# One crossbar transpose per chunk pair of q, in a planned attention and MLP kernel

## The chip, the cores and the metric

The kernel runs on one core of one Trainium2 chip. The metric is device time in microseconds (us) of one launch. The core has a matrix engine (TensorE, PE in the profile, with its weight loads as PEld), a vector engine (DVE), a scalar engine (ACT), GpSimd (POOL), and a sync engine (SP) that here only issues transfers. Sixteen DMA engines move the data. Each engine runs its own instructions strictly in order and waits on semaphores for the others.

## The reference

A block-wise decaying linear attention, followed by a two-layer MLP whose activation is a smooth ReLU. In short:

```
for each block of 64 positions of a sequence (4 batches, 8 heads, 768 positions, head size 64):
    out   = ((q k^T) * lam^(i-j), lower triangle) v  +  (q * lam^(i+1)) state
    state = lam^64 * state + (k * lam^(63-i))^T v
x = out, as (3072 tokens, 512)
h = x @ w_in                        # 512 -> 2048
g = 0 if h <= -1, h if h >= 1, else (h + 1)^2 / 4
y = g @ w_out                       # 2048 -> 512, float32
```

## The kernel before

**Attention.** The kernel works on 24 chunks c of 128 tokens, 6 in each batch, and gathers four chunks into a stripe of 512 tokens, 6 stripes in all. q is loaded for a pair m of chunks at once (`lq`, 512 KB, line 460), with the pair's 256 tokens dealt alternately to two halves e = 0 and 1. k and v are loaded for one chunk at a time (`ld`, 256 KB each, line 464). GpSimd multiplies q and k by powers of lam and casts them to bf16: `cq` (m, e) by `cast_q` (line 244) and `cast` (c, 1) by `cast` (line 240); the casts of k for the first four chunks are on the vector engine. The scalar engine casts v (`cast` (c, 2), line 259).

For the score product, q and k are needed with the head dimension on the partitions. For the first pairs (m below 3) and chunks (c below 6) TensorE transposes them (`tq`, `t`). For the other 9 pairs and 18 chunks a crossbar DMA issued from SP does: `f_qx` (line 288) issues one of 512 columns for each half e of a pair, 18 in all, into `qT`, and `f_kx` (line 284) one for each chunk of k into `kT`, also 18.

Then, for a chunk, TensorE computes the scores `s` (lines 309 to 315), the vector engine masks them (`m`, line 317), and TensorE computes the output `o` (lines 326 to 335) from the masked scores and the running state. `u` (line 291) adds the chunk to the state, from the cast k and v alone. ACT copies the state (`ub`) and the output (`x`, line 337).

**MLP.** `l1` (lines 347 to 368) multiplies a stripe with w_in, `r` (ACT, line 370) and three vector operations `g` (lines 378, 381 and 386) make the activation, and `l2` (line 391) multiplies with w_out: for each of the four chunks `ms` of a stripe, four groups `kg` of four matmuls of 512 columns, accumulated in one tile. `la` are the first four l1 of the first stripe, over the 384 tokens that are there first. `y` (ACT, line 410) copies a finished tile, and `st` (line 427) stores it. The last tile of the kernel is cut into two column parts.

**Order.** Nothing in the order is left to the hardware. All operations are given to a small list planner (`run_plan`, lines 178 to 227) with an estimated duration, the operations that they need, and a due time. It plays the program through by these estimates and writes each engine's instructions in the order that it finds. So a changed estimate, or a changed list of needs, moves instructions on every engine. The estimates are only used for the order. l2 of a stripe is woven between the l1 of the next (lines 430 to 443). For the last stripe there is no next l1, and its sixteen l2 groups run one after another.

**Transfers.** SP issues all loads of q, k and v, all crossbar transposes and all stores through one queue. The weights go through GpSimd's queue (`w`, lines 155 and 159), in eight transfers of 512 KB. By lines 478 to 500 some transfers wait for a weight transfer to land, so the weights and the first chunks take turns.

**Tiles.** `qs` (the cast q) has one tile for each half, from the pool `qkp` with 4 buffers; `ks` has another 4 there. `qT` is one tile for a pair, with 3 buffers. The program tracks which instruction must wait for which by the tiles' addresses.

Of the kernel before, what the change touches and what calls it, by code (L numbers as in the profile page):

```python
# [9 lines left out]
BF16 = mybir.dt.bfloat16  # L10
# [5 lines left out]
def _bc(ap, idx, n):  # L16

    a = list(ap.ap)
    a = a[:idx] + [[0, n]] + a[idx:]
    return bass.AP(ap.tensor, ap.offset, a)  # L20
# [3 lines left out]
def kernel(  # L24
# [16 lines left out]
    nc = tc.nc  # L41
    B, H, S, D = q.shape
# [7 lines left out]
    FO = d_ff // 128  # L50
    MS = 512
    NST = n_tok // MS
    NCH = n_tok // C
    CPS = MS // C

    LD = 6
    LQ, NQ2 = 3, 3
# [13 lines left out]
    lq = ctx.enter_context(tc.tile_pool(name="lq", bufs=LQ))  # L71
    qtq = ctx.enter_context(tc.tile_pool(name="qtq", bufs=NQ2))
    qkp = ctx.enter_context(tc.tile_pool(name="qkp", bufs=NQK))
    qtp = ctx.enter_context(tc.tile_pool(name="qtp", bufs=NQT))
    scp = ctx.enter_context(tc.tile_pool(name="scp", bufs=3))
    xp = ctx.enter_context(tc.tile_pool(name="xp", bufs=3))
# [33 lines left out]
        out=causal, in_=causal, compare_op=AX.is_ge, fill=0.0,  # L110
# [52 lines left out]
    LAT, FILL = 70, 170  # L163
    FAR, SLACK, XSL = 8, 5000, 2000
# [9 lines left out]
    def add(key, eng, ns, fn, needs=(), due=None, extra=0, dma=0, perf=False):  # L174
        OPS[key] = Op(key, eng, ns, fn, needs, due, extra, dma, perf)
        ops.append(OPS[key])

    def run_plan(free):

        users = {x.key: [] for x in ops}  # L180
        for x in ops:
            x.needs = [OPS[y] for y in x.keys if y in OPS]
            for y in x.needs:
                users[y.key].append(x)
        left = {x.key: len(x.needs) for x in ops}
        topo = [x for x in ops if not x.needs]
        for x in topo:
            for u in users[x.key]:
                left[u.key] -= 1
                if left[u.key] == 0:  # L190
                    topo.append(u)
        assert len(topo) == len(ops)
        for x in reversed(topo):
            d = [u.due - u.ns - x.extra - LAT for u in users[x.key] if not u.dma]
            x.due = min(d + ([x.own] if x.own is not None else []), default=1e9)
            if x.dma or x.key[0] in ("l1", "l2"):
                x.due = x.own
        left = {x.key: len(x.needs) for x in ops}
        ready = {e: [] for e in free}
        for x in topo:  # L200
            if not x.needs:
                ready[x.eng].append((0, x))
        out_seq, xfer, dma_free = [], [0] * RING, 0
        while len(out_seq) < len(ops):
            t, e = min((max(free[e], min(r for r, _ in lst), xfer[-RING] if e == "SP" else 0), e)
                       for e, lst in ready.items() if lst)
            r, x = min(((r, x) for r, x in ready[e] if r <= t), key=lambda p: (p[1].due, p[0]))
            ready[e].remove((r, x))
            ns = x.ns + (720 if x.perf and free["POOL"] > t else 0)
            free[e] = t + ns  # L210
            x.t, x.end = t, t + ns + x.extra
            if x.dma:
                dma_free = max(dma_free, t + (1300 if e == "SP" else 2100)) + x.dma
                x.end = dma_free + 1400
                if x.key[0] in ("ld", "lq") and x.key[1] >= (FAR if x.key[0] == "ld" else FAR // 2):
                    x.end += SLACK if (x.key[1] if x.key[0] == "ld" else 2 * x.key[1]) >= 10 else NEAR
                if e == "SP":
                    xfer.append(dma_free)
            out_seq.append((t, len(out_seq), x))
            for u in users[x.key]:  # L220
                left[u.key] -= 1
                if left[u.key] == 0:
                    ready[u.eng].append((max(y.t if y.eng == u.eng and y.key != u.gate else y.end + (XSL if u.eng == "SP" and y.eng == "POOL" and u.dma == 640 else LAT) for y in u.needs), u))
        for t, _, x in sorted(out_seq, key=lambda p: p[:2]):
            if DBG:
                print(f"{t / 1e3:9.3f} {x.due / 1e3:9.3f} {x.eng:5s} {x.ns:6.0f} {x.key}")
            x.fn()

    def mm(*cols):
        return sum(c / 2.4 + 3 for c in cols)  # L230


    qs, ks, kT, qT, sc_sb, xT, ptt, pst, pot = {}, {}, {}, {}, {}, {}, {}, {}, {}
# [8 lines left out]
        eng.tensor_tensor(ks[c], qkv_ld[c, 1], _bc(tab_k[:, c % NCB, :], 2, D), op=AX.mult)  # L242

    def cast_q(m, e, eng):
        qs[m, e] = qkp.tile([128, H, D], BF16, name="qs", tag="qs")
        eng.tensor_tensor(qs[m, e], qkv_ld[m, 0][:, :, e], _bc(tab_q[:, e, m % (NCB // 2), :], 2, D), op=AX.mult)  # L246

    def qT_tile(m):
        if m not in qT:
            qT[m] = qtq.tile([128, 2, HP, 128], BF16, name="qT", tag="qT")  # L250
        return qT[m]
# [33 lines left out]
        kT[c] = qtp.tile([128, HP, 128], BF16, name="kT", tag="kT")  # L285
        nc.sync.dma_start_transpose(out=kT[c], in_=ks[c].rearrange("p h d -> p (h d)"))

    def f_qx(m, e):
        nc.sync.dma_start_transpose(out=qT_tile(m)[:, e], in_=qs[m, e].rearrange("p h d -> p (h d)"))  # L289

    def f_u(c):
        if c % NCB == 0:
# [140 lines left out]
    for s in range(1, NST + 1):  # L433
        n = PARTS.get(s, 1)
        l1 = [(1, s, i, p) for p in range(n) for i in range(0, FO, n)]
        l2 = [(ms, kg) for ms in range(CPS) for kg in range(CPS)]
        if s == 1:
            l2 = [(ms, kg) for kg in range(CPS) for ms in range(2)] + l2[FO // 2:]
        for i in range(FO):
            l_seq.append((2, s - 1) + l2[i])  # L440
            if s < NST:
                l_seq.append(l1[i])
# [26 lines left out]
    def f_w(it, wait):  # L469
        (load_w_in, load_w_out)[it[0]](it[1])  # L470
        if wait is not None:
            tc.add_manual_dep(w_dma[-1].ins, w_dma[wait].ins.name, SYNC)
# [5 lines left out]
    for it in order:  # L478
        if isinstance(it, tuple):
            prev = order[order.index(it) - 1]  # L480
            gated = len(w_seen) - 1 - prev % 2 if w_seen and isinstance(prev, int) else None
            need = [("w",) + w_seen[-1], ("cast", CPS - 1, 1) if len(w_seen) > 1 else None] if w_seen else \
                [("cast", CPS - 2, 2), ("cast", CPS - 2, 1)]
            if gated is not None:
                need.append(("w",) + w_seen[gated])
            add(("w",) + it, "POOL", 900, lambda it=it, wait=gated: f_w(it, wait), need, due=pos_ * 1e-3,
                dma=2560)
            if gated is not None:
                OPS[("w",) + it].gate = ("w",) + w_seen[gated]
            w_seen.append(it)  # L490
            pos_ += 1
            continue
        gated = len(w_seen) - 2 if last_c is not None and w_seen and not isinstance(order[order.index(it) - 1], int) else None
        for x in (1, 2) if it % 2 else (1, 0, 2) if it == 0 else (0, 1, 2):
            need = [("w",) + w_seen[-2] if w_seen else None]
            if x == 0:
                add(("lq", it // 2), "SP", 700, lambda i=it, wait=gated: f_load(i, 0, wait),
                    [("cq", it // 2 - LQ, 0), ("cq", it // 2 - LQ, 1)] + need, due=pos_ * 1e-3, dma=1850)
            else:
                add(("ld", it, x), "SP", 590, lambda i=it, x=x, wait=gated if x == 1 and i % 2 else None: f_load(i, x, wait),  # L500
                    [("cast", it - LD, x)] + need, due=pos_ * 1e-3, dma=1190)
            pos_ += 1
        last_c = it

    for c in range(NCH):
        od, cb = o_due(c), c % NCB
        lastu = c - 1 if cb else c - 2
        m = c // 2
        e = "DVE" if c < CPS else "POOL"
# [4 lines left out]
        for i in range(2 if c % 2 == 0 else 0):  # L514
            old = ("tq", m - NQK // 2, i)
            add(("cq", m, i), "POOL", 1060, lambda m=m, i=i: cast_q(m, i, nc.gpsimd),
                [("lq", m), ("cq", m, 0) if i else None, old, ("qT",) + old[1:]])
            if m < XQ:
                add(("tq", m, i), "PE", mm(*[128] * 4), lambda m=m, i=i: f_tq(m, i),
                    [("cq", m, i)] + ([("kT", c - 1), ("m", c - 1, 1), ("tq", m, 0) if i else None] if c >= CPS else []),  # L520
                    due=od - 6000, extra=FILL)
                add(("qT", m, i), "ACT", 600, lambda m=m, i=i: f_qT(m, i), [("tq", m, i)])
            else:
                add(("qT", m, i), "SP", 1200, lambda m=m, i=i: f_qx(m, i), [("cq", m, i), ("o", 2 * (m - NQ2) + 1)], due=-2, dma=640)
        if c < XT:
            add(("t", c), "PE", mm(*[128] * 4), lambda c=c: f_t(c),
                [("cast", c, 1), ("kT", c - 1), ("kb", c - 1, 0), ("kb", c - 1, 1), ("m", c - 1, 1) if c > 3 else None,
# [1 line left out]
                due=od - 6000, extra=FILL)  # L529
# [33 lines left out]
    for n1, (_, s, i, p) in enumerate(l1_order):  # L563
# [3 lines left out]
        j = (i // n) % rw  # L567
# [12 lines left out]
    for n2, (_, s, ms, kg) in enumerate(l2_order):  # L580
# [5 lines left out]
        y = s * CPS + ms  # L586
        add(("l2", n2), "PE", mm(*[512] * 4) if (s, ms) != LAST else mm(*[CUT if kg < 2 else d_model - CUT] * 8), lambda a=(s, ms, kg): f_l2(*a),
            need + [("w", 1, kg), ("l2", n2 - 1), ("y", y - 2) if kg == 0 else None], due=l_due[2, s, ms, kg], extra=FILL)
        if (s, ms) == LAST:
            if kg % 2:  # L590
                i = kg // 2
# [37 lines left out]
```

## Time and profile before

| | |
|---|---|
| median of 6 runs | 224.32 us (223.78 to 226.22) |
| the profiled execution, its time | 224.35 us |
| its span, first to last instruction | 222.7 us |
| TensorE matmul busy | 206.3 us, 93% |
| vector, scalar, GpSimd busy | 146.3, 124.0, 62.8 us |
| q transposes by DMA | 18, median 4.3 us from issue to landing |
| k transposes by DMA | 18, median 3.5 us from issue to landing |
| loads of k, of q, of v | 24, 12, 24; median 5.2, 5.4, 5.3 us to landing |

The profile has a page of one execution, and answers to queries of its trace. A row of the timeline gives the start in us, the duration, the engine, the line, the operation with the tile written and those read, how many were merged, and in brackets how long the engine had been idle and who ended the wait. "SPq" is SP's queue of transfers; the time of its row is that of issuing, and the landing is told apart. A row of the table of windows gives the busy time of each engine in a stretch, the granted TensorE clock, the mean busy share of the DMA engines, and GB/s. The share can come out a little over 1.

### The profile page before, as it was taken

What the parts mean: (1) busy time and instruction counts of PE and PEld (TensorE: products, weight loads), DVE (VectorE), ACT (ScalarE), POOL (GpSimd) and SP (SyncE); (2) the same over time, 40 slices, a digit from 0 to 9 for tenths busy, and PEclk for the clock granted to TensorE, in tenths of its full rate; (3) what the DMA queues carried; (4) which work ended last, traced back from release to release, by engine and by line L of the source; (5) the groups of instructions that cost most, each with busy time, mean ns of one, the idle gap of its engine ahead of it and who ended that gap; (6) DMA issues with size and microseconds to landing.
All of it is one profiled execution on the core that took longest, in us unless ns stands there. A gap on an engine that the chain in (4) does not pass through costs nothing.

```text
span 222.7 us, 4691 instructions
## 1 busy us (share of the span) xinstructions
PE 206.3 (93%) x1904; PEld 135.9 (61%) x1904; DVE 146.3 (66%) x218; ACT 124.0 (56%) x221; POOL 62.8 (28%) x65
## 2 busy tenths in 40 slices
PE   0587997999998999999999999999999999999993
PEld 0375544668577877776766766777767644444442
DVE  4577299989947875978477659995565564554301
ACT  3464868547547676657657465677645544455120
POOL 7371074217615360915141037520000000000000
PEclk9999999999999999999999999999999999999999
DMA  5999999999699999999999999984101101110212
GB/s 132 242 201 191 188 243 215 183 208 240 102 245 170 200 207 195 174 213 151 218 157 340 213 234 268 187 190 97 65 29 50 43 4 50 47 47 9 85 53 93
DMA packets 89974, 34.40 MB, mean 154 GB/s; under 512 B 70368, under 2 KB 87008, under 8 KB 89952
## 3 DMA queue, kind: packets, MB, share of 16 engines
q1 hardware_dynamic: 85584, 29.89, 66.6%
q0 software_dynamic: 4224, 4.19, 11.7%
q8 instruction: 15, 0.25, 0.5%
q14 instruction: 7, 0.06, 0.1%
q10 hardware_dynamic: 144, 0.00, 0.0%
HBM read 27.27 MB, written 6.29 MB: 151 GB/s over the span
## 4 chain that ended last, share of the span: by engine, by line
PE 67%; DMA 24%; SPq 4%; POOL 2%; issue 1%; DVE 0%; POOLq 0%
PE py L405 30%; PE ph L362 27%; DMA x0f<-in_q_dram 9%; DMA w_out_sb<-in_moe_w_out_dram 7%; DMA w_in_sb<-in_moe_w_in_dram 5%; PE po L334 3%; SPq L464 3%; PE ps L314 2%; DMA kT<-ks 2%; PE po L331 1%; POOL qs L246 1%; PE pu L295 1%; PE py L399 1%; POOL w_in_sb L155 1%; SPq L289 1%
## 5 line engine op out<-in xcount | busy, mean ns | idle before, releaser
L370 ACT ACTIVATE r<-ph,one 128x512 bf16<-128x512 f32 (+2 forms) x96 | 64.8, 679 | 54.3 <-PE ph L362 34.9
L362 PE MATMUL ph<-xT,w_in_sb 128*128 128x128 bf16 (+2 forms) x880 | 94.0, 255 | 0.2 <-ACT r L370 0.2
L405 PE MATMUL py<-w_out_sb,gT 128*128 128x512 bf16 x368 | 92.1, 379 | 0.0
L362 PEld LDWEIGHTS <-w_in_sb 128*128 128x128 bf16 x880 | 65.4, 98 | 23.3 <-issue 1.0
L378 DVE TENSOR_SCALAR t<-r 128x1024 bf16<-128x1024 bf16 x48 | 29.8, 621 | 38.7 <-ACT r L370 38.7
L405 PEld LDWEIGHTS <-gT 128*128 128x128 bf16 x368 | 33.9, 98 | 31.4 <-DVE gT L386 0.2
L386 DVE TENSOR_TENSOR gT<-w,t 128x1024 bf16<-128x1024 bf16 x48 | 40.3, 839 | 1.7
L381 DVE TENSOR_TENSOR w<-r,t 128x1024 bf16<-128x1024 bf16 x48 | 38.3, 797 | 1.3
L246 POOL TENSOR_TENSOR qs<-x0f,tab_q 128x512 bf16<-128x512 f32 x24 | 28.4, 1203 | 33.9 <-DMA x0f<-in_q_dram 29.0
L242 POOL TENSOR_TENSOR ks<-x1f,tab_k 128x512 bf16<-128x512 f32 x20 | 24.5, 1230 | 40.4 <-DMA x1f<-in_k_dram 19.6
L324 DVE TENSOR_TENSOR sc<-ps,causal 128x512 bf16<-128x512 f32 x20 | 13.7, 687 | 12.1 <-PE pt L314 12.1
L410 ACT COPY osb<-py 128x512 f32<-128x512 f32 x23 | 13.5, 586 | 12.3 <-PE py L405 10.4
L341 ACT CAST xT<-po 128x512 bf16<-128x512 f32 x24 | 14.1, 587 | 10.6 <-PE po L334 5.4
L334 PE MATMUL po<-sc,vi 128*128 128x128 bf16 x192 | 18.5, 222 | 0.6 <-DVE sc L322 0.5
L260 ACT CAST vi<-x2f 128x512 bf16<-128x512 f32 x24 | 14.8, 618 | 5.0 <-DMA x2f<-in_v_dram 4.9
L299 ACT CAST ubd<-pu 64x256 bf16<-64x256 f32 x40 | 14.6, 365 | 5.2 <-PE pu L295 4.9
L334 PEld LDWEIGHTS <-vi 128*128 128x128 bf16 x192 | 14.8, 100 | 3.4 <-issue 1.4
L331 PE MATMUL po<-qT,ubd 128*128 128x128 bf16 x80 | 14.6, 219 | 0.5 <-ACT xT L341 0.5
L324 DVE TENSOR_TENSOR sc<-pt,causal 128x512 bf16<-128x512 f32 x20 | 13.6, 680 | 0.0
L265 PE MATMUL pt<-ident,ks 128*128 128x128 bf16 x24 | 2.8, 248 | 7.4 <-DVE ks L242 7.2
L331 PEld LDWEIGHTS <-ubd 128*128 128x128 bf16 x80 | 7.8, 98 | 1.6
L314 PE MATMUL ps<-qT,kT 64*128 64x128 bf16 x80 | 7.9, 219 | 0.9 <-DMA kT<-ks 0.9
(55 smaller groups left out, 87.9 us busy)
## 6 DMA issues: line engine op xcount, KB each, us to landing
x1f<-in_k_dram SPq DMA_DIRECT2D x24, 256.0 KB, 5.2
x0f<-in_q_dram SPq DMA_DIRECT2D x12, 512.0 KB, 5.4
x2f<-in_v_dram SPq DMA_DIRECT2D x24, 256.0 KB, 5.3
out_dram<-osb SPq DMA_DIRECT2D x23, 256.0 KB, 2.5
w_in_sb<-in_moe_w_in_dram POOLq DMA_DIRECT2D x4, 512.0 KB, 9.1
w_out_sb<-in_moe_w_out_dram POOLq DMA_DIRECT2D x4, 512.0 KB, 8.6
qT<-qs SPq DMA_TRANSPOSE x18, 4.3
kT<-ks SPq DMA_TRANSPOSE x18, 3.5
```

The costliest lines, as they stand in the source:

```text
L242: eng.tensor_tensor(ks[c], qkv_ld[c, 1], _bc(tab_k[:, c % NCB, :], 2, D), op=AX.mult)
L246: eng.tensor_tensor(qs[m, e], qkv_ld[m, 0][:, :, e], _bc(tab_q[:, e, m % (NCB // 2), :], 2, D), op=AX.mult)
L260: nc.scalar.copy(out=v_out(vi[c % NV]), in_=qkv_ld[c, 2].rearrange("p (a b) d -> p a b d", b=2))
L324: nc.vector.tensor_tensor(sc_sb[c][:, g], pst[c, g], _bc(causal, 1, HP), op=AX.mult)
L331: nc.tensor.matmul(po[:, hp], lhsT=ubd[(c - 1) % NUB][:, hp, :], rhs=q_cols(c, hp), start=True, stop=False)
L334: nc.tensor.matmul(po[:, hp], lhsT=vi[c % NV][:, hp, hi].rearrange("p a d -> p (a d)"), rhs=sc_sb[c][:, hi, hp, :], start=(cb == 0 and hi ...
L362: nc.tensor.matmul(ph[:, j * m:(j + 1) * m], lhsT=w_in_sb[:, ko, (ni + j) * 128:(ni + j + 1) * 128], rhs=xT[s][:, ko, part * m:(part + 1) ...
L370: nc.scalar.activation(out=r_t[grp][:, i, cs], in_=ph_t[s, ni, part][:, cs], func=AF.Relu, bias=one[:, 0:1])
L378: nc.vector.tensor_scalar(t_t[grp], r, 0.5, 1.0, op0=AX.mult, op1=AX.min)
L381: nc.vector.tensor_tensor(w_t[grp], r, t_t[grp], op=AX.subtract)
L386: nc.vector.tensor_tensor(gT[s][:, f - RW * n:f, part * m:(part + 1) * m], w_t[grp].rearrange("p a (b m) -> p (a b) m", m=m), t_t[grp].rea ...
L405: nc.tensor.matmul(py_t[s, ms], lhsT=gT[s][:, ko, ms * 128:(ms + 1) * 128], rhs=w_out_sb[:, ko, :], start=(ko == 0), stop=(ko == FO - 1))
```

## The change

Four edits are made together.

1. The two halves of a pair's cast q lie in one tile, `qs[m]`, of a new pool `qsp` with 2 buffers. One crossbar DMA of 1024 columns transposes both halves, in place of two of 512. It needs the second half's cast, and is planned with 2000 ns of issue and 1280 ns of transfer, where each of the two had 1200 and 640. The planner's allowance between a GpSimd cast and a transpose of q or k, `XSL`, holds for the new size too.
2. The planner's `need` of the first weight transfer names the cast of the second half of q's pair 1, where it named the casts of k and v of chunk 2. What the transfer itself waits for on the chip is not set by this list.
3. In the last stripe, the first eight l2 groups come in the order (0,0), (0,1), (0,2), (1,0), (1,1), (1,2), (0,3), (1,3), where it was (0,0) to (0,3) and then (1,0) to (1,3).
4. Through the planner, the order of the instructions changes on PE, ACT, DVE and SP. On GpSimd it stays as it was.

```
+    qsp = ctx.enter_context(tc.tile_pool(name="qsp", bufs=2))
...
-... (XSL if u.eng == "SP" and y.eng == "POOL" and u.dma == 640 else LAT) ...
+... (XSL if u.eng == "SP" and y.eng == "POOL" and u.dma in (640, 1280) else LAT) ...
...
     def cast_q(m, e, eng):
-        qs[m, e] = qkp.tile([128, H, D], BF16, name="qs", tag="qs")
+        if e == 0:
+            qs[m] = qsp.tile([128, 2, H, D], BF16, name="qs", tag="qs")
+        qs[m, e] = qs[m][:, e]
...
-    def f_qx(m, e):
-        nc.sync.dma_start_transpose(out=qT_tile(m)[:, e], in_=qs[m, e].rearrange("p h d -> p (h d)"))
+    def f_qx(m):
+        nc.sync.dma_start_transpose(out=qT_tile(m).rearrange("p e h j -> p (e h) j"), in_=qs[m].rearrange("p e h d -> p (e h d)"))
...
+        if s == NST:
+            l2 = [(0, 0), (0, 1), (0, 2), (1, 0), (1, 1), (1, 2), (0, 3), (1, 3)] + l2[FO // 2:]
...
-                [("cast", CPS - 2, 2), ("cast", CPS - 2, 1)]
+                [("cq", CPS // 2 - 1, 1)]
...
-                add(("qT", m, i), "SP", 1200, lambda m=m, i=i: f_qx(m, i), [("cq", m, i), ("o", 2 * (m - NQ2) + 1)], due=-2, dma=640)
+                if i:
+                    add(("qT", m, 1), "SP", 2000, lambda m=m: f_qx(m), [("cq", m, 1), ("o", 2 * (m - NQ2) + 1)], due=-2, dma=1280)
```

More of the change, by code (lines that the diff above doesn't have):

```diff
@@ L222, in run_plan @@
                 if left[u.key] == 0:
-                    ready[u.eng].append((max(y.t if y.eng == u.eng and y.key != u.gate else y.end + (XSL if u.eng == "SP" and y.eng == "POOL" and u.dma == 640 else LAT) for y in u.needs), u))
+                    ready[u.eng].append((max(y.t if y.eng == u.eng and y.key != u.gate else y.end + (XSL if u.eng == "SP" and y.eng == "POOL" and u.dma in (640, 1280) else LAT) for y in u.needs), u))
         for t, _, x in sorted(out_seq, key=lambda p: p[:2]):
```

## The prediction

> **What bounds the kernel now.** I read the page's busy times first, then the table of windows, to see where TensorE is not the bound.
>
> ```profile
> PE 206.3 (93%) x1904; PEld 135.9 (61%) x1904; DVE 146.3 (66%) x218; ACT 124.0 (56%) x221; POOL 62.8 (28%) x65
> ```
> ```profile
> 36.00:60.00 24.00, 23.74 (x250) 15.59 (x250) 21.81 (x30) 14.40 (x27) 10.61 (x10) 1.00 1.05 194
> 60.00:70.00 10.00, 9.28 (x125) 7.02 (x123) 5.64 (x10) 6.05 (x11) 3.36 (x4) 1.00 0.99 181
> 70.00:148.00 78.00, 78.00 (x864) 56.94 (x862) 60.19 (x81) 49.29 (x88) 30.58 (x26) 1.00 1.11 210
> 148.00:205.00 57.00, 57.00 (x390) 33.19 (x389) 32.60 (x53) 30.70 (x51) 1.04 (x1) 1.00 0.18 53
> ```
>
> The first figure is the window's length, the second TensorE's busy time, the last three the granted clock, the DMA engines' share and GB/s. From 70 us on TensorE never idles at the full clock, so time is gained only ahead of that, and lost wherever a new wait appears. The DMA engines are full until about 148 us, so a late landing is the wait to fear. TensorE's timeline gives the idle times that can go, and the instructions that come just after their data:
>
> ```profile
> 20.89 0.27 PE L334 MATMUL po<-sc,vi 128*128 128x128 bf16 x2 [0.50 <-DVE sc L322]
> 34.41 0.38 PE L272 MATMUL pt<-ident,qs 128*128 128x128 bf16 x4 [0.67 <-ACT qT L278]
> 53.31 0.39 PE L295 MATMUL pu<-vi,ks 128*128 128x128 bf16 x4
> 59.40 0.23 PE L314 MATMUL ps<-qT,kT 64*128 64x128 bf16 x1 [0.21 <-DMA kT<-ks]
> 69.43 0.23 PE L314 MATMUL ps<-qT,kT 64*128 64x128 bf16 x1 [0.72 <-DMA kT<-ks]
> 87.07 0.23 PE L314 MATMUL ps<-qT,kT 64*128 64x128 bf16 x1
> ```
>
> These are o(3), the second q transpose of pair 2, u(6), and the scores s(6), s(8) and s(10). GpSimd's timeline shows how close u(6) is to its cast of k, which ends at 51.61 + 1.49 = 53.10:
>
> ```profile
> 49.16 2.49 POOL L246 TENSOR_TENSOR qs<-x0f,tab_q 128x512 bf16<-128x512 f32 x2 [8.93 <-DMA x0f<-in_q_dram]
> 51.61 1.49 POOL L242 TENSOR_TENSOR ks<-x1f,tab_k 128x512 bf16<-128x512 f32 x1
> ```
>
> SP's queue around the first transposes, and two answers on single tiles (q's pair 3, k's chunk 10), give the price of a half and k's slack:
>
> ```profile
> 51.15 2.11 SPq L464 DMA_DIRECT2D x1f<-in_k_dram  x1
> 53.36 3.46 SPq L289 DMA_TRANSPOSE qT<-qs  x2
> 56.91 2.52 SPq L286 DMA_TRANSPOSE kT<-ks  x2
> 59.53 0.53 SPq L464 DMA_DIRECT2D x2f<-in_v_dram  x1
> ```
> ```profile
> L289 SPq DMA_TRANSPOSE qT<-qs x2: 1205/1680/2156, 53.4 to 55.6; - x2
> DMA to landing us min/median/max: 2.6/3.5/4.4
> ```
> ```profile
> L286 SPq DMA_TRANSPOSE kT<-ks x1: 2289/2289/2289, 81.7 to 81.7; - x1
> DMA to landing us min/median/max: 4.5/4.5/4.5
> ```
>
> The two halves land at 53.4 + 4.4 = 57.8 and 55.6 + 2.6 = 58.2, about 0.45 us apart. kT of chunk 10 lands at 86.1, and s(10) starts at 87.07: 0.9 us of slack.
>
> **The change part by part.** The sum is made against the profiled execution, 224.35 us (span 222.7 and 1.65 around it), which is 0.03 above the median.
>
> *The transposes.* A half costs SP 1.21 us of issuing when nothing holds it up, and 128 KB of transfer. One transfer for both isn't in the trace. Its issue lies between one half's 1.21 us (the plain q load, twice k's size, also issues in about k's time) and 2 x 1.21 = 2.4 us and a little more; I take 2.4, since the row nearest is the same instruction. Its transfer lies between 0.45 us (as one half) and twice the longest delay seen for a half; I take 0.9, two halves. So SP and the DMA engines lose nothing and gain at most nine times 1.2 us of issue, which is off the path unless SP starves the DMA engines. It does so at 57 to 61 us: four transposes are issued there in a row, from 53.36 to 59.44, and the share falls to 0.53.
>
> The Trainium skill (DMA: Bandwidth & Descriptors, Rules for kernel authors) says to join many small transfers into one, with a fixed cost of some 2.0 us each (Anatomy of one DMA). By that rule nine transfers fewer would be up to 18 us less; the 0.45 us between the landings of two halves says that the fixed parts already overlap, and by it the gain is nothing.
>
> *The wait for the second half.* The transpose now needs both casts. For pair 3 they end at 51.65, before SP comes to it at 53.36: nothing. A pair's first cast must now wait until the whole tile of two pairs before has been read: pair 5's cast starts at 68.0, when pair 3 has been landed for nearly 10 us: nothing.
>
> *The first weight transfer.* GpSimd's order doesn't move, and on the chip the transfer already follows the cast of q directly (14.44). It starts no earlier: 0. But the planner thinks so, and writes other orders:
>
> *Start.* la(0) goes ahead of o(3), and l1(11) between the two q transposes of pair 2. They fill the idle 0.50 and 0.67 us. Most is taken back: u(6) needs the cast of k at 53.10, which hangs on the chain of weight landings and q's load, and none of these moves. With the 0.04 us that TensorE needs after a release, u(6) can start at 53.14, 0.17 earlier. If GpSimd's three operations ran unslowed at 1.04 instead of up to 1.49, the cast would end at 52.3 and TensorE would keep some 1.0 us. The vector engine is as busy there as before, so I take 0.3, near the lower end.
>
> *s(6).* SP now issues the load of v for chunk 8 ahead of the transposes, which fills the hole at 57 to 61. It adds about 1.1 us ahead of pair 3's transpose. That lands at about 59.4, then kT(6) behind it at 59.8. But l2 groups 11 and 12 now come ahead of s(6), 2 x 0.86 = 1.73 us. TensorE comes to it at 59.19 - 0.17 + 1.73 = 60.7. The 0.21 us go, with 0.9 us to spare; if the big transfer needs the full 2 us more, 1 us comes back.
>
> *s(8).* Three l2 and two l1 groups now come ahead of it, 3 x 0.86 + 2 x 0.89 = 4.4 us. Ahead of kT(8) stand two more loads, 2.2 us, less the hole that was filled. It lands at about 70.3, where TensorE comes at 69.43 - 0.93 - 0.17 + 4.4 = 72.7. The 0.72 us go with over 2 us to spare. u(8) moves about 6 us forward, to about 61.9; its cast of k ended at 60.3, its load of v is now the one in front.
>
> *What is late next: s(10).* TensorE comes to it 1.1 to 1.2 us earlier, at 85.9, and kT(10) was there at 86.1. The same loads stand ahead of kT(10) in both orders, so it is earlier only by holes filled: 57 to 61 held 4 x (1.05 - 0.53) = 2 us of them, a good part of which goes. I take 1 us or more: no wait. If nothing is gained there, 0.3 us come back. s(20) has the same slack of 1.2 us (it starts at 147.63, kT was issued at 144.0 and took 2.4), and two loads now stand ahead of its kT; the DMA lead must cover them.
>
> *s(18) and s(19).* A vector operation on r now comes ahead of the two masks of chunk 18. In the trace the masks ended at 144.01, and s(19), which reuses their PSUM tiles, started at 144.57. The operation takes 0.43 to 1.29 us: 0 to 0.7 us come back; I take 0.1, from its undisturbed length.
>
> *Last stripe.* The group that needs the last activation moves from fourth to seventh place. From 205.02 the 48 matmuls run in 10.4 us, 0.216 each, so no wait is there to remove. The third chunk now needs the first's copied tile after one other group: copy 0.59 us and about 0.2 to start against 0.86. Cost 0 to 0.1: nothing.
>
> Sum: 224.35 - 0.3 - 0.21 - 0.72 + 0.1 = 223.2 us.
>
> **The rivals.**
>
> *Given back at s(10) or s(20).* The DMA lead does not come about, and the kernel ends 0.9 us earlier at most, at s(10)'s slack: 223.5, or nearly the old time if s(20) and the masks take some more. For it speaks that the DMA engines are saturated; against it the hole at 57 to 61.
>
> *The big transfer is slower than two halves (slower than before).* If it takes d longer, and the DMA engines are full, each later load and kT is d later per pair. Up to s(10) three pairs count, against some 2 us of lead and slack together: from d = 0.7 us on, TensorE waits there. At d = 1 that is 1 us, and up to s(20), with eight pairs, about 4 us more: 224.35 - 1.1 + 5 = 228. Against it: the packets to be moved are the same bytes, and a half shows no fixed part in its spacing. For it: no such transfer is in the trace, and a pair elsewhere took longer to land (5.6 us at 76.4).
>
> *The cast at u(6) is early.* Then the filled idle times stay: 224.35 - 1.0 - 0.93 = 222.4.
>
> **How the numbers follow.** The forecast with its bounds (222.7 to 223.6) has 0.48, the early cast 0.08, the gain given back 0.20, the slower transfer 0.24. Half a per cent, 1.12 us, is about what a measurement of this kernel can tell from no change. Faster than that: three quarters of the forecast's case and all of the early cast's and a little of the third, 0.46. Within it: 0.30. Slower: 0.24. The range for 8 in 10 reaches from the early cast, 222.2, into the slower case, 226.2; the likeliest case alone has 222.7 to 223.6.
>
> **What would show it.** Right: nine transposes of q with about 2.4 us of issue; no idle time at s(6) and s(8); a new idle time of about 1 us shared between u(4) and u(6), on GpSimd's cast; TensorE whole from there on. Wrong: idle time ahead of scores after 80 us with a late kT (the lead, or the big transfer), pairs that land more than 1 us later than their halves did, or a wait of scores on the masks near 143 us.

## The result and the profile after

The changed kernel takes 223.78 us in the median, the kernel before 224.89 us beside it: a ratio of 0.994, with a 95% interval of 0.9924 to 0.9957. Measured twice more, on other chips, it came to 0.9964 (0.9931 to 0.9997) and 0.9948 (0.9914 to 0.9981). The forecast was 223.2 against 224.35, a ratio of 0.995. The profiled execution took 223.83 us, 0.52 less than that of before.

First the page's busy times of the changed kernel, and its table of windows, with the columns as before:

```profile
PE 206.1 (93%) x1904; PEld 135.8 (61%) x1904; DVE 145.5 (66%) x218; ACT 123.6 (56%) x221; POOL 63.0 (28%) x65
```
```profile
36.00:60.00 24.00, 22.40 (x231) 15.07 (x232) 19.94 (x28) 12.77 (x23) 10.23 (x10) 1.00 1.03 198
60.00:70.00 10.00, 10.00 (x118) 6.91 (x117) 4.99 (x8) 5.50 (x11) 3.20 (x4) 1.00 0.95 198
70.00:148.00 78.00, 77.74 (x877) 57.28 (x875) 62.69 (x85) 50.07 (x90) 32.71 (x27) 1.00 1.13 211
```

The idle time of 0.72 us between 60 and 70 us is gone, and TensorE lost more than before between 36 and 60 us. TensorE's timeline names the places: u(4), u(6), the l1 group behind it, s(6), s(8), s(10) and s(20).

```profile
34.16 0.40 PE L298 MATMUL pu<-vi,ks 128*128 128x128 bf16 x4 [0.79 <-POOL ks L243]
...
53.49 0.38 PE L298 MATMUL pu<-vi,ks 128*128 128x128 bf16 x4 [1.40 <-ACT vi L263]
54.08 1.05 PE L365 MATMUL ph<-xT,w_in_sb 128*128 128x128 bf16 x16 [0.21 <-ACT r L373]
...
61.36 0.23 PE L317 MATMUL ps<-qT,kT 64*128 64x128 bf16 x1
...
73.25 0.23 PE L317 MATMUL ps<-qT,kT 64*128 64x128 bf16 x1
...
86.79 0.23 PE L317 MATMUL ps<-qT,kT 64*128 64x128 bf16 x1 [0.21 <-DMA kT<-ks]
...
147.47 0.23 PE L317 MATMUL ps<-qT,kT 64*128 64x128 bf16 x1
```

The start did become faster: the scores of chunk 4, s(4), stood at 37.01 us and stand at 35.60. Then u(6), which started at 53.31, starts at 53.49, so all 1.41 us are given back there, to a load of v that landed at 52.8 (51.4 before) and the scalar engine's cast of it. The waits at s(6) and s(8) are gone; s(10) has a new one of 0.21. The last l2 groups start at 204.85 against 205.02. Another 0.4 us lie at the very end: the span ends 2.9 us after the vector engine's last copy, against 3.3 before.

SP's timeline around the first transposes, and the answer on q's last transpose alone, where little stands ahead of it:

```profile
53.62 1.15 SPq L469 DMA_DIRECT2D x2f<-in_v_dram  x1
54.88 2.82 SPq L292 DMA_TRANSPOSE qT<-qs  x1
57.79 2.52 SPq L289 DMA_TRANSPOSE kT<-ks  x2
60.40 0.53 SPq L469 DMA_DIRECT2D x1f<-in_k_dram  x1
```
```profile
L292 SPq DMA_TRANSPOSE qT<-qs x1: 1283/1283/1283, 147.4 to 147.4; - x1
DMA to landing us min/median/max: 3.2/3.2/3.2
```

The load of v for chunk 8 now stands ahead of the transposes. The 1024 columns took SP 2.82 us at 54.88, where three loads issued before had not landed yet, but 1.28 us at 147.4, where one transfer was under way: about the price of one half (1.21), not of two.

### The profile page after: what moved, and what is told of

Its sections match the earlier page's. It is cut to its first block, busy times and chain, and to the rows that moved or that the text cites. A ratio compares the mean times of both kernels' runs of the same rounds, so it can differ in the third digit from the quotient of the medians.

```text
span 222.1 us, 4660 instructions
## 1 busy us (share of the span) xinstructions
PE 206.1 (93%) x1904; PEld 135.8 (61%) x1904; DVE 145.5 (66%) x218; ACT 123.6 (56%) x221; POOL 63.0 (28%) x65
## 4 chain that ended last, share of the span: by engine, by line
PE 64%; DMA 24%; POOL 4%; SPq 3%; issue 3%; ACT 0%; DVE 0%; POOLq 0%
PE py L408 31%; PE ph L365 24%; DMA x2f<-in_v_dram 7%; DMA w_in_sb<-in_moe_w_in_dram 5%; DMA x0f<-in_q_dram 5%; DMA kT<-ks 4%; PE po L337 3%; DMA w_out_sb<-in_moe_w_out_dram 3%; SPq L469 3%; PE ps L317 2%; POOL qs L249 2%; PE po L334 1%; PE py L402 1%; POOL ks L243 1%; POOL w_in_sb L156 1%
## 5 line engine op out<-in xcount | busy, mean ns | idle before, releaser
L381 DVE TENSOR_SCALAR t<-r 128x1024 bf16<-128x1024 bf16 x48 | 28.1, 584 | 40.0 <-ACT r L373 39.9
L389 DVE TENSOR_TENSOR gT<-w,t 128x1024 bf16<-128x1024 bf16 x48 | 40.8, 849 | 1.6
L243 POOL TENSOR_TENSOR ks<-x1f,tab_k 128x512 bf16<-128x512 f32 x20 | 25.0, 1254 | 30.4 <-DMA x1f<-in_k_dram 13.2
L298 PE MATMUL pu<-vi,ks 128*128 128x128 bf16 x80 | 8.2, 228 | 2.4 <-ACT vi L263 1.4
L298 PEld LDWEIGHTS <-ks 128*128 128x128 bf16 x80 | 6.1, 102 | 5.0 <-POOL ks L243 2.6
```

The lines of the kernel that those rows point to most:

```text
L381: nc.vector.tensor_scalar(t_t[grp], r, 0.5, 1.0, op0=AX.mult, op1=AX.min)
L389: nc.vector.tensor_tensor(gT[s][:, f - RW * n:f, part * m:(part + 1) * m], w_t[grp].rearrange("p a (b m) -> p (a b) m", m=m), t_t[grp].rea ...
```

## The experiments

Two theories stood against each other at first. Mine: the gain is the new order, above all the loads that fill the DMA engines at 57 to 61 us, and the waits at s(6) and s(8); the transfer itself is worth nothing. The rival: the transfer itself matters.

**One edit at a time.** Only the single transpose, with its figures for the planner (the lists of the other two edits as before):

```
+ f_qx(m): one transpose of qs[m] into qT_tile(m); planner: 2000 ns, dma=1280
  need of the first weight transfer: as before;  l2 of the last stripe: as before
```

> Before plus the single 1024-column transpose alone (with its planner figures); the list of needs and the last stripe stay as before. SP's order, and l2 groups 11, 12 ahead of s(6) and l2 and l1 groups ahead of s(8), come as in the changed kernel; the start stays as before. Theory (the gain is the two waits at s(6) and s(8)): no idle time there, 0.9 us less, perhaps 0.1 to 0.4 of it lost again at s(10), s(20) and the masks: 0.996 to 0.998 of before. Rival (the gain comes from the order at the start): 0.999 to 1.001. Rival (the big transfer is slower than two halves): above 1.000, with late kT after 80 us.

Measured: 0.9945 (0.991 to 0.998), a larger gain than the theory had said (0.996 to 0.998). No idle time at s(6), s(8), s(10) or s(20) in its profile. So this edit, with the order that the planner makes of it and the old start, gives by itself all that the four edits together give, as far as these intervals tell.

Only the list of needs:

```
-                [("cast", CPS - 2, 2), ("cast", CPS - 2, 1)]
+                [("cq", CPS // 2 - 1, 1)]
```

> Before plus the changed list of needs of the first weight transfer alone: the order of TensorE up to u(6) as in the changed kernel, SP's order and the two transposes as before. Theory: the start gains about 1.1 to 1.4 us at o(3) and at q's second transpose of pair 2, but s(6) and s(8) still wait for kT(6) at about 59.4 and kT(8) at about 69.4, which hang on SP and the loads; so all is given back at u(6) or s(6), 0.999 to 1.001 of before, and the idle time ahead of s(6) or u(6) grows by what the start gained. Rival (the start's gain is kept): 0.993 to 0.996.

Measured: 0.9983 (0.995 to 1.0016). Its TensorE rows are u(6), s(8) and two l1 groups:

```profile
53.47 0.38 PE L295 MATMUL pu<-vi,ks 128*128 128x128 bf16 x4 [0.52 <-ACT vi L260]
...
70.31 0.23 PE L314 MATMUL ps<-qT,kT 64*128 64x128 bf16 x1 [1.16 <-DMA kT<-ks]
...
113.62 1.03 PE L362 MATMUL ph<-xT,w_in_sb 128*128 128x256 bf16 x8 [0.80 <-ACT r L370]
134.26 1.03 PE L362 MATMUL ph<-xT,w_in_sb 128*128 128x256 bf16 x8 [0.45 <-ACT r L370]
```

What the start gained is given back, and two further waits appear that the profile of before did not have: the activation of an l1 group is late, because the scalar engine stood at a cast of v whose load was late.

Only the order in the last stripe, and, the other way round, the changed kernel without it:

```
+        if s == NST:
+            l2 = [(0, 0), (0, 1), (0, 2), (1, 0), (1, 1), (1, 2), (0, 3), (1, 3)] + l2[FO // 2:]
```

> Before plus the new order of the first eight l2 groups of the last stripe alone. Theory: nothing, 0.999 to 1.001; TensorE's last 80 matmuls take the same time to 0.05 us. Rival (the profile of the changed kernel ends 2.9 us after its last vector operation against 3.3 before, and the reorder is what made it so): 0.998.

> The changed kernel with the last stripe's l2 in the old order; all else, and the order of every engine ahead of the last stripe, as in the changed kernel. Theory (the new order there is worth nothing): the same ratio as the changed kernel run beside it, to 0.2%, and TensorE takes 14.0 us from the first of its last 80 matmuls to its end in both. Rival (the new order costs 0.3%, as the run of that edit alone has it): 0.3% faster than the changed kernel beside it.

Measured: 1.0029 (1.0005 to 1.0052) with the edit alone; the changed kernel without it 0.9977 (0.995 to 1.0004), with the changed kernel beside it at 0.9964. The two signs contradict each other. From the start of the last stripe's l2 to the start of the first column part TensorE took 10.36 us in all four profiles (205.02 to 215.38 before, 206.98 to 217.34 with the edit alone, 206.86 to 217.22 without it in the changed kernel, 203.98 to 214.34 in a second profile of the changed kernel). The order is worth nothing there. The 0.3% of the edit alone have no mechanism in the trace: ahead of 205 us that kernel issues the same instructions as before, but in its profile the loads came later, and so did the waits:

```profile
70.65 0.23 PE L314 MATMUL ps<-qT,kT 64*128 64x128 bf16 x1 [1.13 <-DMA kT<-ks]
...
113.75 1.03 PE L362 MATMUL ph<-xT,w_in_sb 128*128 128x256 bf16 x8 [0.51 <-ACT r L370]
```

So the profile of before that the forecast was made from was a good execution. In it, v of chunk 17 landed at 109.7 us, and TensorE did not wait behind the scalar engine's cast of it; here it landed at 112.5 and cost TensorE 0.51 us.

**The transfer by itself.** The changed kernel in its whole order, with two transposes of 512 columns in place of each of 1024:

```
-        nc.sync.dma_start_transpose(out=qT_tile(m)..., in_=qs[m]...)
+        for e in range(2):
+            nc.sync.dma_start_transpose(out=qT_tile(m)[:, e], in_=qs[m, e]...)
```

> The changed kernel in its whole order, but where it issues one transpose of 1024 columns this issues the two of 512, one behind the other. Theory (the gain is the order, the transfer itself is worth nothing): 0.993 to 0.996 of before, as the changed kernel. Rival (the single transfer saves SP and the DMA engines time): 0.997 or more, with kT later by 0.5 us or more per pair. Rival (the single transfer is slower than two halves): below 0.993.

Measured: 1.0255 (1.0212 to 1.0298). My theory fell; the rival that the single transfer saves time holds. The table of windows of this kernel, and then of the changed kernel's third profile (its first has shares of 1.11 and 1.13 there); the last two figures are the DMA engines' share and GB/s:

```profile
85.00:100.00 15.00, 14.25 (x189) 11.10 (x190) 9.71 (x16) 8.75 (x16) 5.62 (x5) 1.00 0.92 161
100.00:115.00 15.00, 12.18 (x142) 8.70 (x142) 8.54 (x12) 6.95 (x15) 5.12 (x4) 1.00 0.79 172
```
```profile
85.00:100.00 15.00, 14.84 (x191) 11.04 (x190) 13.30 (x16) 9.76 (x18) 6.87 (x6) 1.00 1.14 205
100.00:115.00 15.00, 14.84 (x160) 11.08 (x158) 11.99 (x15) 8.98 (x16) 7.16 (x6) 1.00 1.15 190
```

The DMA engines do less per us with two halves, not more. SP's rows at the pair of chunks 14 and 15 show why; first the kernel with two halves, then the changed kernel (third profile):

```profile
105.58 2.90 SPq L293 DMA_TRANSPOSE qT<-qs x2
108.59 2.51 SPq L289 DMA_TRANSPOSE kT<-ks  x2
```
```profile
99.30 2.20 SPq L292 DMA_TRANSPOSE qT<-qs  x1
101.60 3.57 SPq L289 DMA_TRANSPOSE kT<-ks  x2
```

k's transposes come 7.0 us later (4.9 against the first profile, 103.66). The lag grows from pair to pair. Against the first profile it is 0.1 us the other way ahead of the first pair (k's load for chunk 8), and at the first transpose of k in pairs 3 to 7 it is 1.2, 1.4, 3.3, 4.4 and 4.9 us. While four transposes are issued in a row, 1.2 us each, 128 KB each are moved in about 0.45 us, and the engines run dry: at 110.8 us, when the last two at this pair are on their way, nothing older is. What TensorE then waits for are s(10) (0.59 us), an activation behind the cast of a late v, and s(20):

```profile
115.72 1.03 PE L366 MATMUL ph<-xT,w_in_sb 128*128 128x256 bf16 x8 [3.44 <-ACT r L374]
...
118.24 1.91 PE L366 MATMUL ph<-xT,w_in_sb 128*128 128x256 bf16 x8
...
154.82 0.23 PE L318 MATMUL ps<-qT,kT 64*128 64x128 bf16 x1 [1.52 <-DMA kT<-ks]
```

Not all of the loss is waiting. After the 3.44 us of standstill, eight l1 matmuls take 1.91 us (the row at 118.24) where the same number took 1.03 in the row above it, and the table of windows shows the granted clock at 0.50:

```profile
117.00:120.00 3.00, 3.00 (x12) 1.67 (x12) 2.96 (x3) 0.48 (x1) 2.32 (x2) 0.50 1.61 173
```

Between 115.72 and 120.87 us TensorE does four groups that take 0.87 us each elsewhere, so the clock costs about 1.7 us there. The waits remain the larger part: of the six runs, the one with a mean clock of 1.00 took 230.18 us, the others 230.51 to 232.95.

**SP's time or the transfer?** The second half adds 1.2 us of SP's issue, but also 128 KB in a transfer of their own. First attempt to part the two: the second half issued by the scalar engine.

```
+        for e, eng in enumerate((nc.sync, nc.scalar)):
+            eng.dma_start_transpose(out=qT_tile(m)[:, e], in_=qs[m, e]...)
```

> The changed kernel with two transposes of 512 columns per pair in place of one of 1024, but the second half is issued by the scalar engine, not by SP. The order is otherwise the same. Theory (what the two halves cost is SP's time: 1.2 us of issue for the second, for which SP's loads behind it come later): SP's stream is as early as in the changed kernel, kT(14) lands near 106 and not 111 us; the scalar engine pays nine times 1.2 us, or more where it waits for a cast, so 0.993 to 1.010 of before, well below the 1.0255 of two halves on SP. Rival (two transfers cost the DMA engines more than one does): kT(14) lands at 109 us or later, and 1.02 or more.

Measured: 1.1445 (1.1392 to 1.1497). It tells nothing on the question, since both expectations missed what happened. The scalar engine's rows:

```profile
53.71 0.37 ACT L303 CAST ubd<-pu 64x256 bf16<-64x256 f32 x1
68.95 1.28 ACTq L293 DMA_TRANSPOSE qT<-qs  x1
70.28 0.37 ACT L303 CAST ubd<-pu 64x256 bf16<-64x256 f32 x1 [16.21 <-DMA x1f<-in_k_dram]
```

The engine stood for 15 us until SP's transpose of k for chunk 8 had landed (68.81), although its data was there. SP in its turn issued k's transpose for chunk 9 only at 72.66 us, when this one had landed. The built program lets no transpose of one queue start before those of the other queue that come ahead of it have landed; the Trainium skill (DMA: Bandwidth & Descriptors, Rules for kernel authors) demands just that for transposes on two queues. This run shows what it costs here, though a part of the 14% is TensorE's clock, whose mean was 0.94 to 0.95 in these runs.

Second attempt: the single transpose, and behind it three loads of 64 bytes, on SP.

```
+        for i in range(3):
+            n = 3 * (m - XQ) + i
+            nc.sync.dma_start(out=tiny[0:1, 16 * n:16 * n + 16], in_=q[0, 0, n:n + 1, 0:16])
```

> The changed kernel, where SP issues three loads of 64 bytes behind each transpose of 1024 columns, into a scratch tile that nobody reads. A plain load costs SP 0.4 to 0.6 us of issue and moves next to nothing here, so this adds 1.2 to 1.7 us of SP's time per pair, as the second half does, without its 128 KB. Theory (the two halves cost what they do by SP's time, during which the DMA engines run dry): the loads and kT behind come 3 to 6 us later by the pair of chunks 14 and 15 (kT(14) at 109 to 112 us against 105.4 to 106.2), with waits at s(10), s(20) and for v(17), and 1.015 to 1.03 of before. Rival (it is the transfer of the halves that costs): kT(14) within 1.5 us of the changed kernel, and below 1.003.

Measured: 1.0359 (1.0307 to 1.041), above the 1.015 to 1.03 of the theory, with the changed kernel beside it at 0.9948. SP's rows at the same pair, and the windows:

```profile
103.92 3.47 SPq L293 DMA_TRANSPOSE qT<-qs  x1
107.44 1.11 SPq L296 DMA_DIRECT2D tiny<-in_q_dram  x3
108.65 2.50 SPq L290 DMA_TRANSPOSE kT<-ks  x2
```
```profile
85.00:100.00 15.00, 13.34 (x173) 10.18 (x173) 10.12 (x16) 8.61 (x16) 6.04 (x5) 1.00 0.95 160
100.00:115.00 15.00, 12.29 (x144) 8.81 (x144) 6.96 (x11) 6.54 (x14) 4.52 (x4) 1.00 0.82 165
```

192 bytes per pair do what 128 KB did: k's transposes at 108.65 against 108.59, shares of 0.95 and 0.82 against 0.92 and 0.79. So the bytes are not the price. (The mean clock was 0.985 to 0.993 in these runs, so here too a part of the time is the clock.) It stayed open whether it is SP's time or a fixed cost of a transfer, whoever issues it; hence the same three loads from the scalar engine:

```
-            nc.sync.dma_start(out=tiny[...], in_=...)
+            nc.scalar.dma_start(out=tiny[...], in_=...)
```

> The kernel with the three loads of 64 bytes per pair, but the scalar engine issues them, at the same places of the program. The DMA engines get the same transfers, and SP's queue is as in the changed kernel. Theory (SP's issue time is the price): the transposes of k for chunks 14 and 15, issued at 108.65 us in the run with the tiny loads on SP and at 101.6 and 103.7 in two profiles of the changed kernel, start between 101 and 104.5; the scalar engine pays 27 x 0.3 us, some of it ahead of TensorE, so 0.994 to 1.010 of before. Rival (each further transfer costs the DMA engines or the queue a fixed time, whoever issues it): 107 us or later, and above 1.02.

Measured: 1.0451 (1.0393 to 1.0508), outside what the theory had said (0.994 to 1.010). The scalar engine's rows and SP's:

```profile
60.74 5.62 ACTq L296 DMA_DIRECT2D tiny<-in_q_dram  x3
66.40 0.37 ACT L306 CAST ubd<-pu 64x256 bf16<-64x256 f32 x1 [11.42 <-DMA x0f<-in_q_dram]
```
```profile
97.56 2.30 SPq L293 DMA_TRANSPOSE qT<-qs  x1
99.98 7.94 SPq L290 DMA_TRANSPOSE kT<-ks  x2
```

The program takes its eight transfer semaphores in turn, and a transfer waits for the last user of its own; the first small load so waited for SP's transpose of k at 60.7 us, the scalar engine stood for 11.4 us, and TensorE waited 9.2 us behind it. The time is therefore no answer. SP's stream is one, up to pair 7: with the same small transfers in the DMA engines it comes to q's transpose at 97.56 us, where it came at 103.92 with them in SP's queue and at 99.30 and 100.94 in the changed kernel. So up to there the transfers by themselves held nothing up, which leaves SP's issue as the price in the run before. A wait for a semaphore is not the price with two halves on SP: there every transfer was issued more than 2.9 us after the last user of its semaphore had landed. Behind pair 7's transpose of q, the second transpose of k waits as well (the row's 7.94 us), and nothing more can be read.

**What is given back at u(6).** The changed kernel, with later landings told to the planner for the loads from chunk 6 on:

```
-    FAR, SLACK, XSL = 8, 5000, 2000
-    NEAR = 2500
+    FAR, SLACK, XSL = 6, 5000, 2000
+    NEAR = 1500
```

> The changed kernel, where the planner takes every load of k and v from chunk 6 on (chunk 8 before), and of q from pair 3 on, to land later than its transfer alone says, by 1.5 us up to chunk 9 (2.5 us before). u(6) comes one l2 group (0.86 us) later, and the scalar engine's cast of v(6) later too; s(8) one group earlier. Theory (what the start gained is given back at u(6)): up to 0.9 us less idle time ahead of u(6), 0.2 to 0.9 us faster than the changed kernel beside it: 0.990 to 0.995 of before. Rival (the next load or kT takes it back): the same as the changed kernel, with the idle time at u(7), s(6), s(8) or s(10).

Measured: 0.9946 (0.9916 to 0.9976), with the changed kernel beside it at 0.9964: no difference that the measurement shows. In its profile u(6) waits only 0.30 us, but 0.33 us stand at s(6), 0.94 and 0.31 us at activations behind a late v, and 0.97 us at s(20). This is what the rival said: the stream of loads takes it back.

**The changed kernel again**, for its spread:

> The changed kernel once more, unaltered, for a second profile of it and for times on the same chip as the three below. In its first profile u(6) waited 1.40 us for the cast of v, whose load landed at 52.8 us. Theory (the landing of the loads between 44 and 55 us differs from execution to execution, and u(6) stands close behind it): 0.993 to 0.997 of before, and an idle time ahead of u(6) that differs from 1.40 by some tenths or more, with the landing of v(6). Rival (the wait at u(6) is a fixed part of the order): 1.3 to 1.5 us again, landing at 52.7 to 52.9.

> The changed kernel unaltered, beside the two above: 0.993 to 0.998 of before; an idle time ahead of u(6) between 0.5 and 1.5 us, ahead of s(10) and s(20) between 0 and 1.5 us.

Measured: 0.9964 and 0.9948. At u(6) 0.58 and 0.44 us idle (1.40 in the first profile; v of chunk 6 landed at 52.1 and 51.9 us, against 52.8). At s(20) none in the second, and in the third:

```profile
147.52 0.23 PE L317 MATMUL ps<-qT,kT 64*128 64x128 bf16 x1 [1.00 <-DMA kT<-ks]
```

The changed kernel without the reorder of the last stripe, the same up to there, waited 1.63 us at s(20). These places differ from execution to execution, with the loads.

**The same for k.** If SP's issue time is the price, k's eighteen transposes can become nine as well.

```
     def cast(c, eng):                       # for c >= XT
-        ks[c] = qkp.tile([128, H, D], ...)
+        if c % 2 == 0:
+            ks["p", c // 2] = ksp.tile([128, 2, H, D], ...)     # bufs=3
+        ks[c] = ks["p", c // 2][:, c % 2]
...
-            add(("t", c), "SP", 1200, ..., [("cast", c, 1), ("m", c - NQT, 1)], due=-2, dma=640)
+            add(("t", c), "SP", 2000, ..., [("cast", c, 1), ("m", c - 6, 1) ...], due=-2, dma=1281)   # odd c only
```

The figure 1281 keeps the allowance XSL from holding for it, so that it goes close behind q's.

> The changed kernel with the same done for k: the casts of two chunks from chunk 6 on lie in one tile, and one transpose of 1024 columns does for both, nine in place of eighteen of 512; the planner gives it 2000 ns, and it goes in SP's order close behind q's. Theory (SP's time is what the stream of loads hangs on): nine times 1.2 us of issue less, so the stream gains up to 1 us per pair until the loads are held by their buffers; the waits at s(10), s(20) and for v(17) go in every execution, the idle time ahead of u(6) stays (it lies ahead of the first transpose): 0.990 to 0.995 of before, 0.2 to 1.0 us faster than the changed kernel beside it. Rival (an even chunk's scores now wait for the odd chunk's load and cast): idle time ahead of s(8) or s(10) of 1 us or more, and not faster than the changed kernel.

Measured: 222.79 us, 0.9876 (0.9835 to 0.9917), with the changed kernel beside it at 224.07 us, 0.9948. It beats both kernels, the changed one by 1.3 us, a little more than had been expected. Its SP rows at the first pair, two transposes where before had four:

```profile
52.51 0.84 SPq L477 DMA_DIRECT2D x2f<-in_v_dram  x1
53.45 2.65 SPq L300 DMA_TRANSPOSE qT<-qs  x1
56.20 1.25 SPq L297 DMA_TRANSPOSE kT<-ks  x1
57.54 0.54 SPq L477 DMA_DIRECT2D x1f<-in_k_dram  x1
```

Behind 55 us its TensorE has no wait of 0.2 us or more for data, at s(10), s(20) or any activation. Ahead of that, 0.72 us at u(4) stay, and u(6) starts at 52.41, earlier than in any profile of the changed kernel. This fits the price of SP's issue but does not part it from two other things that change here: the planner writes another order, and the cast and the transposed k have room for six chunks each where they had room for four.

## Why the prediction came out right, and where it did not

The time and the sign were right, and the two waits at s(6) and s(8) went as described. Their sizes: TensorE came to s(6) at 61.36 and to s(8) at 73.25, forecast 60.7 and 72.7; kT(6) and kT(8) landed at 60.4 and 71.4, forecast 59.8 and 70.3. The rest of the sum has to be corrected.

- *"So SP and the DMA engines lose nothing and gain at most nine times 1.2 us of issue, which is off the path unless SP starves the DMA engines. It does so at 57 to 61 us ..."* This is the step that failed. The issue was taken at 2.4 us; unhindered it is 1.28 us, the lower bound. And SP starves the engines at more than one place: with two halves in the new order, their share falls to between 0.37 and 0.57 for 2 us at or behind each of the five groups of transposes between 55 and 115 us, and in the kernel of before to 0.56 to 0.65 at 69, 95 and 105 us as well. In the new order the second half costs some 3% (1.0255 against 0.994 to 0.9964), 6.5 to 7.1 us, or 0.7 to 0.8 us for each of nine, the 1.7 us of lowered clock included. Why most of that is not seen as a gain is not shown, since no run has one transpose for a pair in the old order; the likely reason is that the order of before was made for a slower stream of loads. The DMA engines' mean share, about 1.1 there in the kernel of before, hid that SP, which only issues, was the bound for some us at a time.
- *The second half's 128 KB*, taken at 0.45 us of transfer, are not the price at all: three loads of 64 bytes cost as much.
- *The rival of the slower transfer* fell. One transfer of 1024 columns landed 3.2 us after its issue; the two halves of the same pair, issued at 154.7 and 156.0 us and landing 2.4 to 2.5 us later, took 3.7 us from the first issue. So d, the prediction's extra time of the big transfer, is about -0.5 us.
- *The start* (0.3 taken): right in size, if by few profiles. u(6) started at 53.31, 53.54 and 54.20 us in three profiles with the old start, and at 53.47, 53.49, 52.78, 53.21 and 53.99 in five with the new one, means of 53.7 and 53.4. (Three profiles with the new start but other transposes or small loads have 53.55, 52.56 and 53.14.) The idle time of u(4) and u(6) together, about 1 us by the forecast, was 2.19, 1.31 and 1.49 us in the changed kernel. What ends the wait was named too narrowly: it is the cast of k, as forecast, or that of v, whichever load is late.
- *s(10) and s(20)* (no wait taken; rival with 0.20): both occur, in some executions: 0.21, 0.16 and 0 us at s(10), 0, 0 and 1.00 at s(20).
- *The masks* (0.1 lost): no such wait was seen in any profile of the changed kernel.
- *The last stripe* (nothing): as forecast.
- *Not in the sum at all:* in the four profiles of kernels with two halves on SP the span ends 3.25 to 3.34 us after the last copy, in the six where only q has one transpose, and no small loads are added, 2.89 to 2.98. So about 0.35 us of the gain lie behind the last copy. What sets them is not shown; with k in pairs it is 2.5 us, with the small loads 2.8.

Where the gain is, by the profiles: the waits of 0.15 us and more behind 55 us add up to 0.93, 1.64 and 2.57 us in three profiles with two halves in the old order, and to 0, 0.21, 0.16, 1.00 and 2.03 in five with the single transpose (the one with later landings, whose order differs, has 2.55), means of 1.7 and 0.7. With 0.3 at u(6) and 0.35 at the end that makes 1.65 us, beside the measured 1.35 (0.97 to 1.7, from the ratio's interval). The forecast had 0.93 there because its one profile had 0.93: the size agreed by luck, since the changed kernel does not remove all of its waits, and the two other profiles with two halves in the old order had more, and since the 0.35 us at the end were not in the sum at all.

The Trainium skill's advice (DMA: Bandwidth & Descriptors, Rules for kernel authors) to make one large transfer of several small ones held, against what the forecast made of the 0.45 us between two landings. Its fixed 2.0 us per transfer (Anatomy of one DMA) is given there for transfers issued from GpSimd, while these are issued from SP, and it is not what was saved: 0.7 to 0.8 us per transpose in the same order.

## What to carry to other kernels

A queue's issue time is a resource like an engine: where transfers are small, add up their issue rows (1.2 us for each of four transposes, against 0.45 us of moving) and see whether the DMA engines' share falls there. A transfer of twice the size in one issue saved SP nearly all of the second issue (1.28 us against twice 1.21), so issues on a queue that feeds the kernel are worth joining even where the bytes stay the same. And a sum made from one profile needs a second one: waits on loads moved by up to 1.6 us between executions of the same instructions.

## What was not expected of the hardware

- A crossbar transpose of 1024 columns (256 KB) cost SP 1.28 us to issue, one of 512 columns 1.21.
- A load of 64 bytes cost SP 0.25 us (three in 1.11 us), and 27 of them 4.1% of the kernel's time (1.0359 against 0.9948), because of where they stood in the queue, the lowered clock included.
- Small transfers on a second queue were not free either: through the shared semaphores they tied the scalar engine to SP's stream, 11.4 us in one place.
- After TensorE had stood for 3.44 us, it was granted half its clock from 117 to 120 us, so a wait cost more than its length.
